# Attention over a key-value cache with a gated MLP: code order, head output and the place of one product

## The chip, the cores and the metric

The kernel runs on one core of a Trainium2 chip. The metric is the device time of one launch in microseconds (us), as the median of several runs. A profiled execution gives the trace that all views below come from.

## The reference

A decode step for two sequences (B = 2), one new token each, D = 512. Cut to what matters:

```python
xn = layernorm(x)
q  = (xn @ wq)                              # 32 query heads of 128
k, v = repeat(k_cache, 4), repeat(v_cache, 4)   # 8 kv heads, 32768 keys of 128
p  = softmax(q @ k.T * 128**-0.5)
s  = (p @ v) @ wo                           # [2, 1, 512]
h  = xn + shifted(gelu(layernorm(xn) @ w1)) @ w2
g  = silu(h + gelu(layernorm(h) @ w3) @ w4)
out = x + s * g
```

With one token per sequence the shifts fill everything with zeros, so the kernel needs neither w1 nor w2. All inputs are bf16. The caches are by far the largest: 8 MB of keys and 8 MB of values for each of the 16 pairs of a sequence and a kv head.

## The kernel before

The work goes in 16 groups, one for each pair (sequence, kv head). A group has four query heads. Its keys come in two halves (slots) of 128 partitions by 128 keys by 128 numbers; `kbuf` has three slots, `vbuf` two. SyncE issues all large transfers on one queue in a fixed order: the keys of the next group when the first half of this group's keys is used up (semaphore `s_half`), the values of the next group when this group's PV has ended (`s_pv`). After the last values come three parts of wo (`wo_parts`: heads 0-3, 4-6, 7), which land in `kbuf` beside the last keys.

The orders of the engines are written out by hand, and semaphores join them; `take` waits for a semaphore and counts it down. In a group:

- VectorE transposes the keys in 16 pieces into four buffers `T` (L481). A fifth transpose waits until TensorE has used the first buffer (`t_used`).
- TensorE multiplies each piece with the query in `z` (L550, 64 products into the banks `sc`).
- VectorE takes the peaks of the scores (`peak`, L464, L466), TensorE spreads them (L562), VectorE gives the negative shift (L493, L495), ScalarE the two exponentials with their sums `rs` (L411), VectorE transposes them into `pt` (L502) and puts the sums into `sm` (L499).
- TensorE adds the sums over the partitions (L566, a product with ones, `S`); then VectorE makes the denominators `den` and their reciprocals `rec` (L506, L510).
- TensorE multiplies the probabilities with the values (PV, L575, 64 products into `o`). Its result lies in four strips, with four blocks of columns in each.

The output of a head is made during the next group. `head_ob` on VectorE, after the fourth transpose, picks the right block of `o` with a mask `row_t` (L442) and adds the four blocks (L446) into `obm`; `head_oT` on TensorE (L526) turns it with one fp32 product; `head_on` on VectorE (L438) divides; `head_xp` on TensorE (L531) spreads it; `head_out` on VectorE (L451, L457, L458) makes a column of `oX`. The start of `head_ob` is released by SyncE (`t_o`), after it has issued the next values.

TensorE runs the 16 turns as a loop in its instruction stream with a counter `turn`. Its code consists of blocks, in memory in this order: `pe_turn` (a branch), `pe_groups` (a turn), `pe_prologue` (queries, MLP), `pe_next` (counts and branches back), `pe_output`. The output stage has the last head's `head_oT`, the 64 products of heads 0-3 with wo (L599), `head_xp`, and the 64 products of heads 4-7. Between the first 64 and `head_xp` it has a branch on `turn` whose target is named ahead by a prefetch hint at the stage's start (L586, L590). VectorE then multiplies with the gate and adds x (L517, L518), and SyncE and ScalarE store the result (L520). VectorE's 16 groups are a loop as well, two groups to a turn.

Of the kernel before, what the change touches and what calls it, by code (L numbers as in the profile page):

```python
# [7 lines left out]
F32 = mybir.dt.float32  # L8
# [86 lines left out]
def kernel(  # L95
# [43 lines left out]
    def sb(name, shape, dt):  # L139
        return pool.tile(shape, dt, name=name)  # L140
# [12 lines left out]
    den = sb("den", [128, rep], F32)  # L153
    obm = sb("obm", [128, Dh], F32)
    mx = sb("mx", [128, NPART], F32)
# [17 lines left out]
    sel_o = sb("sel_o", [128, VT, rep], F32)  # L173
    row_t = sb("row_t", [128, VT], F32)
    quad = sb("quad", [128, 4], BF16)
# [37 lines left out]
    def sem(name):  # L213
        return tc.alloc_semaphore(name)
# [14 lines left out]
    t_used, t_top, t_e, t_S, t_oT, t_xp = (sem(f"t_{n}") for n in ("used", "top", "e", "S", "oT", "xp"))  # L229
    t_d, t_o = sem("t_d"), sem("t_o")  # L230
    t_k = [sem(f"t_k{i}") for i in range(NPART)]
# [14 lines left out]
    with tc.tile_critical(no_gpsimd_drain=True):  # L246
# [15 lines left out]
        e_z0 = po.op(lambda e: e.memset(z[:, :, :, :], 0.0))  # L262
        e_g0 = po.op(lambda e: e.memset(g4[:, :], 0.0))
        for n in range(NQ):
            ac.op(lambda e, n=n: e.dma_start(out=x4_bf[32 * n:32 * n + B, :], in_=A_x[:, 0, n * QW:(n + 1) * QW]), e_x4z, inc=(d_x4, 16))


        ve.op(lambda e: e.memset(o[:, :], 0.0), inc=(t_o, 1))
        ve.op(lambda e: e.memset(pro[:, :], 0.0))
# [21 lines left out]
        for j in range(4):  # L291
# [5 lines left out]
            axis=AX.X, op=ALU.add))  # L297
        ve.op(lambda v: v.tensor_reduce(out=row_t[:, :], in_=sel_o[:, :, :], axis=AX.X, op=ALU.add), (ve.sem, ve.n))
        with nc.allow_low_precision(reason="one of the terms is one, the others are zero"):
# [88 lines left out]
        for m in range(1, NG):  # L388
            base = m % 2
            if m < NG - 1:  # L390
                sp.op(lambda e, m=m, base=base: e.dma_start(
                    out=kbuf[:, base * SLOT:(base + NPART) * SLOT], in_=row_view(A_k_cache, *groups[m])),
                    (s_half, m), e_q, inc=(t_k[0], 16))
                nc.sync.sem_inc(t_k[1], 16)
            else:
                for i, h in enumerate(order(m)):
                    sp.op(lambda e, m=m, h=h, base=base: e.dma_start(
                        out=kbuf[:, (base + h) * SLOT:(base + h + 1) * SLOT],
                        in_=row_view(A_k_cache, *groups[m])[:, h * SLOT:(h + 1) * SLOT]),
                        (s_half, m), inc=(t_k[i], 16))  # L400
            load_v(m, (s_pv, m))
            nc.sync.sem_inc(t_o, 1)
        for i, (a, c) in enumerate(wo_parts):
            sp.op(lambda e, a=a, c=c: e.dma_start(out=wo3[:, a:c, :], in_=wos[:, a:c, :]), (s_pv, NG - 1), inc=(d_wo[i], 16))
        sp.wait((s_pv, NG))
        nc.sync.sem_inc(t_o, 1)


        for m in range(NG):
            for i in range(NPART):  # L410
                ac.op(lambda v, i=i: v.activation(  # L411
                    out=ep[i][:, :], in_=sc[i][:, :], func=ACT.Exp, scale=inv_sqrt_dh, bias=shift[:, :], accum_out=rs[:, i:i + 1]),
                    (s_shift, m + 1), e_tf if m == 0 else None, inc=(t_e, 1))

        z_cols = z[:, :, :, (NR - 1) * rep:].rearrange("p n e c -> p (n e) c")
# [19 lines left out]

        def head_on():
            take(nc.vector, t_oT, 2)
            nc.vector.tensor_mul(out=on[:, :], in0=oT[:, :], in1=rec[:, :]).then_inc(t_on, 1)  # L438

        def head_ob():  # L440
            take(nc.vector, t_o)
            nc.vector.tensor_mul(  # L442
                out=ob[:, :].rearrange("p (t d) -> p t d", t=VT), in0=o[:, :].rearrange("p (t d) -> p t d", t=VT),
                in1=row_t[:, :].unsqueeze(2).broadcast_to([128, VT, Dh])).then_inc(t_d, 1)
            take(nc.vector, t_d)
            nc.vector.tensor_reduce(  # L446
                out=obm[:, :], in_=ob[:, :].rearrange("p (t d) -> p d t", t=VT), axis=AX.X, op=ALU.add).then_inc(t_ob, 1)

# [20 lines left out]

        ve.op(lambda v: v.memset(rec[:, :], 1.0), inc=(t_oT, 1))  # L470
        with nc.Fori(0, NG // 2, engines=[DVE], hint_back_edge=True):
            for par in range(2):
                for i, h in enumerate(order(par)):
# [3 lines left out]
                    for r in range(NR):  # L477
                        n = i * NR + r
                        if n >= T_BUFS:
# [3 lines left out]
                            in_=kt[:, r * W:(r + 1) * W].rearrange("p (t b k) -> p t b k", b=NB, t=RT)).then_inc(t_T, 1)  # L483
                        if i == 0 and r == 3:
                            head_ob()
                        if i == 1 and r == 3:
# [9 lines left out]
                for i, h in enumerate(order(par)):  # L496
                    take(nc.vector, t_e)
                    if i == NPART - 1:
# [5 lines left out]
                        in_=ep[i][:, :].rearrange("p (t r h) -> p t r h", r=NR, h=rep)).then_inc(t_pt, 1)  # L504
                take(nc.vector, t_S)
                nc.vector.tensor_reduce(  # L506
                    out=den[:, :], in_=S[:, 0:NPART * rep].rearrange("p (i h) -> p h i", h=rep),
                    axis=AX.X, op=ALU.add).then_inc(t_d, 1)
                take(nc.vector, t_d)
                nc.vector.reciprocal(out=rec[:, :], in_=den[:, :]).then_inc(t_oT, 1)  # L510
        head_ob()
        head_on()
# [11 lines left out]
        def head_oT():  # L524
            take(nc.tensor, t_ob)
            nc.tensor.matmul(oT[:, :], lhsT=obm[:, :], rhs=sel_h[:, :], start=True, stop=True).then_inc(t_oT, 1)  # L526

# [13 lines left out]
        with nc.body("pe_groups", valid_engines=[PE]):  # L541
            take(nc.tensor, t_z)
            for i in range(NPART):
# [21 lines left out]
            take(nc.tensor, t_pt, NPART)  # L565
            nc.tensor.matmul(  # L566
                S[:, 0:NPART * rep], lhsT=ones_f[:, :], rhs=sm[:, :, :].rearrange("p i h -> p (i h)"),
                start=True, stop=True).then_inc(t_S, 1)
            for h in range(NPART):
# [11 lines left out]
            ins.then_inc(s_pv, 1)  # L581
            nc.br("pe_next", engines=[PE])


        with nc.body("pe_output", valid_engines=[PE]):
            in_next_block = nc.tensor.mark_branch_hint_location()  # L586
            head_oT()
            for i, (a, c) in enumerate(wo_parts):
                if i == 1:
                    nc.tensor.br_ne(turn, 0, "pe_output_2", "pe_turn").branch_hint(in_next_block)  # L590
                    nc.switch_bb("pe_output_2")
                    head_xp()
# [13 lines left out]
        with nc.body("pe_prologue", valid_engines=[PE]):  # L606
            prologue.place()
            for s, v in prologue._new((e_s00, e_ones, e_const, e_hf, e_tf)):
                nc.tensor.wait_ge(s, v)
            nc.br("pe_next", engines=[PE])  # L610
        with nc.body("pe_next", valid_engines=[PE]):
            nc.regs_alu(turn, turn, 1, op=ALU.add)
            nc.br_lt(turn, NG + 1, on_true="pe_turn", on_false="pe_output", engines=[PE])
        nc.regs_mov(turn, 0)
# [32 lines left out]
```

## Time and profile before

| what | value |
|---|---|
| median of 3 runs | 661.88 us (661.82 to 662.24) |
| the profiled execution, its own time | 662.16 us |
| its span, first to last instruction | 660.0 us |
| mean granted TensorE clock | 0.828 |
| TensorE busy with products | 423.8 us (64%) |
| VectorE busy | 404.0 us (61%) |
| ScalarE busy | 29.6 us (4%) |
| moved by DMA | 280.57 MB, mean 425 GB/s |

The span is the time from the first to the last instruction that the profile shows; the profiled execution's own time is 2.16 us longer. Views give times in us from the start of the span. "Lnnn" is a line of the kernel before. An idle time stands with what ended it ("<-"); "issue" means that the engine waited for nothing that the profile shows. PEld is TensorE's weight load, and an engine's name with a q (SPq, DVEq) its sequencer.

### The profile page before, as it was taken

The numbers are of one execution on the slowest core, as the hardware profiler recorded it, in microseconds if no ns is written. First come the engines' busy times: TensorE is split into PE (matmuls) and PEld (weight loads), VectorE is DVE, ScalarE is ACT, GpSimd is POOL, SyncE is SP. The second block draws the span as 40 slices with busy tenths as digits, with TensorE's granted clock in tenths as the row PEclk, the third lists the DMA queues.
The fourth block names the chain that finished last, engine by engine and source line by source line (L and its number), as shares of the span: only waits on it lengthen the run. The fifth ranks groups of instructions, "written<-read, shape, count | busy, mean of one in ns | idle before, by whom it ended". The sixth has DMA issues, their size and how long they took to land. (4 is left out here: it accounts for less than half of the span.)

```text
span 660.0 us, 6591 instructions
## 1 busy us (share of the span) xinstructions
PE 423.8 (64%) x2412; PEld 151.6 (23%) x2412; DVE 404.0 (61%) x571; ACT 29.6 (4%) x72; POOL 9.7 (1%) x42
## 2 busy tenths in 40 slices
PE   1637396666739666684965668496566848656965
PEld 0112132222213222221321222132122213212323
DVE  5349293773929477392946739294673919468761
ACT  1100000000000000000000000000000000000000
POOL 1000000000000000000000000000000000000000
PEclk9859788796978879697877969677796977779897
DMA  8999999999999999999999999999999999999994
GB/s 361 442 438 441 445 437 421 417 445 441 445 433 417 425 445 441 441 429 422 429 445 441 441 421 429 429 445 441 437 425 429 429 445 441 433 425 419 435 414 167
DMA packets 6458, 280.57 MB, mean 425 GB/s; under 512 B 682, under 2 KB 692, under 8 KB 1716
## 3 DMA queue, kind: packets, MB, share of 16 engines
q1 hardware_dynamic: 6408, 280.50, 98.3%
q8 instruction: 2, 0.03, 0.0%
q14 instruction: 4, 0.03, 0.0%
q10 hardware_dynamic: 44, 0.01, 0.0%
HBM read 280.50 MB, written 0.00 MB: 425 GB/s over the span
## 5 line engine op out<-in xcount | busy, mean ns | idle before, releaser
L481 DVE STREAM_TRANSPOSE T<-kbuf 128x1024 int32<-128x1024 int32 x256 | 293.9, 1210 | 151.7 <-DVEq L461 151.7
L550 PE MATMUL sc<-T,z 128*128 128x512 bf16 x1024 | 295.8, 424 | 137.1 <-PEq L461 128.2
L550 PEld LDWEIGHTS sc<-T,z 128*128 128x128 bf16 x1024 | 92.6, 103 | 325.8 <-issue 268.0
L575 PE MATMUL o<-vbuf,pt 128*16 128x512 bf16 x1024 | 92.7, 542 | 0.0
L411 ACT ACTIVATE ep<-sc,shift 128x512 bf16<-128x512 f32 x32 | 21.7, 683 | 581.0 <-DVE shift L495 581.0
L575 PEld LDWEIGHTS o<-vbuf,pt 128*16 128x16 bf16 x1024 | 30.8, 119 | 54.2 <-issue 47.2
L566 PE MATMUL S<-sm,ones_f 128*128 128x8 f32 x32 | 9.0, 354 | 51.8 <-PEq L461 51.8
L502 DVE STREAM_TRANSPOSE pt<-ep 128x512 bf16<-128x512 bf16 x32 | 22.6, 708 | 15.3 <-DVEq L461 15.3
L464 DVE TENSOR_REDUCE mx<-sc 128x1 f32<-128x512 f32 x32 | 21.5, 672 | 15.7 <-DVEq L461 15.7
L562 PE MATMUL S<-mxr,same_h 128*128 128x64 f32 x32 | 6.5, 284 | 22.0 <-PEq L461 22.0
L566 PEld LDWEIGHTS S<-sm,ones_f 128*128 128x128 f32 x32 | 7.9, 307 | 53.5 <-issue 53.5
L446 DVE TENSOR_REDUCE obm<-ob 128x128 f32<-128x512 f32 x17 | 17.7, 1040 | 2.5
L442 DVE TENSOR_TENSOR ob<-o,row_t 128x512 f32<-128x512 f32 x17 | 11.2, 656 | 7.6 <-DVEq L461 7.6
L562 PEld LDWEIGHTS S<-mxr,same_h 128*128 128x128 f32 x32 | 4.8, 188 | 29.8 <-issue 29.8
L506 DVE TENSOR_REDUCE den<-S 128x4 f32<-128x8 f32 x16 | 2.7, 167 | 13.7 <-DVEq L461 13.7
L466 DVE TENSOR_SCALAR mxr<-row_of,mx 128x32 f32<-128x32 f32 x32 | 7.7, 241 | 4.8
L431 POOL COPY oX<-oXs 128x4 bf16<-128x4 bf16 x15 | 2.9, 191 | 517.6 <-DVE oXs L458 517.6
L493 DVE TENSOR_REDUCE top<-S 128x1 f32<-128x64 f32 x16 | 3.6, 224 | 11.2 <-DVEq L461 11.2
L526 PEld LDWEIGHTS oT<-sel_h,obm 128*128 128x128 f32 x34 | 6.3, 188 | 5.4 <-issue 2.7
L329 PE MATMUL sc<-kbuf,xT 128*2 128x512 bf16 x32 | 3.6, 627 | 5.5 <-DMA kbuf<-in_A_wq_dram 5.5
L366 PE MATMUL sc<-vbuf,h_bf 128*2 128x512 bf16 x14 | 4.9, 522 | 2.4 <-DVE h_bf L363 2.4
L420 POOL TENSOR_TENSOR z<-qr,quad 128x64 bf16<-128x64 bf16 x16 | 4.7, 294 | 107.6 <-DVE shift L495 90.4
(80 smaller groups left out, 73.8 us busy)
## 6 DMA issues: line engine op xcount, KB each, us to landing
kbuf<-in_A_k_cache_dram SPq DMA_DIRECT2D x2, 4096.0 KB, 22.0
vbuf<-in_A_v_cache_dram SPq DMA_DIRECT2D x2, 4096.0 KB, 18.6
kbuf<-in_A_wq_dram SPq DMA_DIRECT2D x1, 4096.0 KB, 13.5
vbuf<-in_B_w_dram SPq DMA_DIRECT2D x2, 1792.0 KB, 19.2
kbuf<-in_A_wo_dram SPq DMA_DIRECT2D x1, 2048.0 KB, 27.6
kbuf<-in_A_wo_dram SPq DMA_DIRECT2D x1, 1536.0 KB, 31.0
kbuf<-in_A_wo_dram SPq DMA_DIRECT2D x1, 512.0 KB, 31.7
kbuf<-in_A_k_cache_dram SPq DMA_DIRECT2D x15, 27.0
```

What stands on the lines that cost most here:

```text
L411: ac.op(lambda v, i=i: v.activation(out=ep[i][:, :], in_=sc[i][:, :], func=ACT.Exp, scale=inv_sqrt_dh, bias=shift[:, :], accum_out=rs[:, i ...
L442: nc.vector.tensor_mul(out=ob[:, :].rearrange("p (t d) -> p t d", t=VT), in0=o[:, :].rearrange("p (t d) -> p t d", t=VT), in1=row_t[:, :]. ...
L446: nc.vector.tensor_reduce(out=obm[:, :], in_=ob[:, :].rearrange("p (t d) -> p d t", t=VT), axis=AX.X, op=ALU.add).then_inc(t_ob, 1)
L464: nc.vector.tensor_reduce(out=mx[:, i:i + 1], in_=sc[i][:, :], axis=AX.X, op=ALU.max).then_inc(t_d, 1)
L466: ins = nc.vector.tensor_scalar_mul(out=mxr[:, i, :], in0=row_of[:, :], scalar1=mx[:, i:i + 1])
L481: nc.vector.transpose(out=Ts[n % T_BUFS][:, :].rearrange("p (b t k) -> p t b k", b=NB, t=RT), in_=kt[:, r * W:(r + 1) * W].rearrange("p (t ...
L502: nc.vector.transpose(out=pt[h][:, :, :].rearrange("p r (t h) -> p t r h", h=rep), in_=ep[i][:, :].rearrange("p (t r h) -> p t r h", r=NR, ...
L526: nc.tensor.matmul(oT[:, :], lhsT=obm[:, :], rhs=sel_h[:, :], start=True, stop=True).then_inc(t_oT, 1)
L550: ins = nc.tensor.matmul(sc[i][:, :], lhsT=z[:, nb, w, zc:zc + 128], rhs=Tb[:, nb, :, w], start=(r == 0 and nb == 0 and w == 0), stop=(r = ...
L562: nc.tensor.matmul(S[:, NPART * rep:], lhsT=same_h[:, :], rhs=mxr[:, :, :].rearrange("p i r -> p (i r)"), start=True, stop=True).then_inc( ...
L566: nc.tensor.matmul(S[:, 0:NPART * rep], lhsT=ones_f[:, :], rhs=sm[:, :, :].rearrange("p i h -> p (i h)"), start=True, stop=True).then_inc( ...
L575: ins = nc.tensor.matmul(o[32 * j:32 * j + VT * rep, :], lhsT=pt[h][:, r, a * VT * rep:(a + 1) * VT * rep], rhs=vt[:, u * VT:(u + 1) * VT, ...
```

## The change

TensorE's blocks are put in another order: the counting and the branch back stand at the end of `pe_groups`, `pe_output` follows, and the prologue comes last, ending with a count and a jump to `pe_turn`. The branch with its hint in the output stage is taken out.

The head's output goes another way: ScalarE copies all of `o` into `ob` as soon as PV has ended, and `head_oT` adds the four blocks with four fp32 products against the selection matrix `sel_o`. `head_ob`, `obm`, `row_t` and the semaphore `t_o` go, and SyncE's increments of it.

The sum of the exponentials (`S`) comes behind PV instead of ahead of it, and VectorE makes `den` and `rec` in `head_on`, in the next group, right before they are used. For the first group `S` and `ob` are filled by memsets.

```diff
+        po.op(lambda e: e.memset(ob[:, :], 0.0), inc=(t_ob, 1))
...
-        ve.op(lambda e: e.memset(o[:, :], 0.0), inc=(t_o, 1))
+        ve.op(lambda e: e.memset(o[:, :], 0.0))
+        ve.op(lambda e: e.memset(S[:, 0:NPART * rep], 1.0), inc=(t_S, 1))
...
-        ve.op(lambda v: v.tensor_reduce(out=row_t[:, :], in_=sel_o[:, :, :], axis=AX.X, op=ALU.add), (ve.sem, ve.n))
...
             load_v(m, (s_pv, m))
-            nc.sync.sem_inc(t_o, 1)
...
-        sp.wait((s_pv, NG))
-        nc.sync.sem_inc(t_o, 1)
...
+            ac.op(lambda v: v.copy(out=ob[:, :], in_=o[:, :]), (s_pv, m + 1), inc=(t_ob, 1))
...
         def head_on():
+            take(nc.vector, t_S)
+            nc.vector.tensor_reduce(
+                out=den[:, :], in_=S[:, 0:NPART * rep].rearrange("p (i h) -> p h i", h=rep),
+                axis=AX.X, op=ALU.add).then_inc(t_d, 1)
+            take(nc.vector, t_d)
+            nc.vector.reciprocal(out=rec[:, :], in_=den[:, :]).then_inc(t_oT, 1)
             take(nc.vector, t_oT, 2)
             nc.vector.tensor_mul(out=on[:, :], in0=oT[:, :], in1=rec[:, :]).then_inc(t_on, 1)
-
-        def head_ob():
...
-        ve.op(lambda v: v.memset(rec[:, :], 1.0), inc=(t_oT, 1))
...
-                        if i == 0 and r == 3:
-                            head_ob()
...
-                take(nc.vector, t_S)
-                nc.vector.tensor_reduce(
-                    out=den[:, :], in_=S[:, 0:NPART * rep].rearrange("p (i h) -> p h i", h=rep),
-                    axis=AX.X, op=ALU.add).then_inc(t_d, 1)
-                take(nc.vector, t_d)
-                nc.vector.reciprocal(out=rec[:, :], in_=den[:, :]).then_inc(t_oT, 1)
-        head_ob()
         head_on()
...
         def head_oT():
             take(nc.tensor, t_ob)
-            nc.tensor.matmul(oT[:, :], lhsT=obm[:, :], rhs=sel_h[:, :], start=True, stop=True).then_inc(t_oT, 1)
+            for t in range(VT):
+                ins = nc.tensor.matmul(
+                    oT[:, :], lhsT=ob[:, t * Dh:(t + 1) * Dh], rhs=sel_o[:, t, :],
+                    start=(t == 0), stop=(t == VT - 1))
+            ins.then_inc(t_oT, 1)
...
             take(nc.tensor, t_pt, NPART)
-            nc.tensor.matmul(
-                S[:, 0:NPART * rep], lhsT=ones_f[:, :], rhs=sm[:, :, :].rearrange("p i h -> p (i h)"),
-                start=True, stop=True).then_inc(t_S, 1)
...
             ins.then_inc(s_pv, 1)
-            nc.br("pe_next", engines=[PE])
+            nc.tensor.matmul(
+                S[:, 0:NPART * rep], lhsT=ones_f[:, :], rhs=sm[:, :, :].rearrange("p i h -> p (i h)"),
+                start=True, stop=True).then_inc(t_S, 1)
+            nc.regs_alu(turn, turn, 1, op=ALU.add)
+            nc.br_lt(turn, NG + 1, on_true="pe_turn", on_false="pe_output", engines=[PE])
...
         with nc.body("pe_output", valid_engines=[PE]):
-            in_next_block = nc.tensor.mark_branch_hint_location()
             head_oT()
             for i, (a, c) in enumerate(wo_parts):
                 if i == 1:
-                    nc.tensor.br_ne(turn, 0, "pe_output_2", "pe_turn").branch_hint(in_next_block)
-                    nc.switch_bb("pe_output_2")
                     head_xp()
...
-            nc.br("pe_next", engines=[PE])
-        with nc.body("pe_next", valid_engines=[PE]):
             nc.regs_alu(turn, turn, 1, op=ALU.add)
-            nc.br_lt(turn, NG + 1, on_true="pe_turn", on_false="pe_output", engines=[PE])
+            nc.br("pe_turn", engines=[PE])
```

More of the change, by code (lines that the diff above doesn't have):

```diff
@@ L153 @@
     den = sb("den", [128, rep], F32)
-    obm = sb("obm", [128, Dh], F32)
     mx = sb("mx", [128, NPART], F32)
@@ L173 @@
     sel_o = sb("sel_o", [128, VT, rep], F32)
-    row_t = sb("row_t", [128, VT], F32)
     quad = sb("quad", [128, 4], BF16)
@@ L229 @@
     t_used, t_top, t_e, t_S, t_oT, t_xp = (sem(f"t_{n}") for n in ("used", "top", "e", "S", "oT", "xp"))
-    t_d, t_o = sem("t_d"), sem("t_o")
+    t_d = sem("t_d")
     t_k = [sem(f"t_k{i}") for i in range(NPART)]
@@ L436, in head_on @@
         def head_on():
+            take(nc.vector, t_S)
[4 more added lines that the diff above has]
+            nc.vector.reciprocal(out=rec[:, :], in_=den[:, :]).then_inc(t_oT, 1)
             take(nc.vector, t_oT, 2)
             nc.vector.tensor_mul(out=on[:, :], in0=oT[:, :], in1=rec[:, :]).then_inc(t_on, 1)
-        def head_ob():
[L441 to L444, printed above, removed]
-            take(nc.vector, t_d)
-            nc.vector.tensor_reduce(
-                out=obm[:, :], in_=ob[:, :].rearrange("p (t d) -> p d t", t=VT), axis=AX.X, op=ALU.add).then_inc(t_ob, 1)
         def head_out(last=False):
@@ L504 @@
                         in_=ep[i][:, :].rearrange("p (t r h) -> p t r h", r=NR, h=rep)).then_inc(t_pt, 1)
-                take(nc.vector, t_S)
-                nc.vector.tensor_reduce(
-                    out=den[:, :], in_=S[:, 0:NPART * rep].rearrange("p (i h) -> p h i", h=rep),
-                    axis=AX.X, op=ALU.add).then_inc(t_d, 1)
-                take(nc.vector, t_d)
-                nc.vector.reciprocal(out=rec[:, :], in_=den[:, :]).then_inc(t_oT, 1)
-        head_ob()
         head_on()
```

## The prediction

> **What bounds the kernel now.** I read the page's DMA rows first, then SyncE's waits and the transfers by line, then the chain that ended last, then the time line of the last 50 us.
>
> ```profile
> DMA  8999999999999999999999999999999999999994
> GB/s 361 442 438 441 445 437 421 417 445 441 445 433 417 425 445 441 441 429 422 429 445 441 441 421 429 429 445 441 437 425 429 429 445 441 433 425 419 435 414 167
> q1 hardware_dynamic: 6408, 280.50, 98.3%
> q8 instruction: 2, 0.03, 0.0%
> ```
>
> The 16 DMA engines are busy in every slice but the last; 280.5 MB at some 430 GB/s are the time. Only what comes after the transfers, or what lets them pause, can move the end. (q8's two packets of 16 KB come back below.)
>
> ```profile
> SPq L380 <- PE o L575: 303.2, 14, 22.4
> SPq L391 <- PE sc L550: 209.1, 13, 16.8
> L380 SPq DMA_DIRECT2D vbuf<-in_A_v_cache_dram x15: 327/328/334, 30.2 to 577.8; - x15
> DMA to landing us min/median/max: 23.6/24.3/31.3
> L404 SPq DMA_DIRECT2D kbuf<-in_A_wo_dram x3: 388/507/4286, 618.5 to 619.5; - x3
> DMA to landing us min/median/max: 27.6/31.0/31.7
> ```
>
> A group's V is issued when the group before has ended its PV. Groups follow each other every 38.6 us, 19.3 us per 8 MB load, and the shortest issue-to-landing of V is 23.6 us: each V load stands at least 4.3 us in a queue that still has work (K: 26.9 - 19.3 = 7.6 us). So in steady state nothing that an engine does counts unless it delays a V issue by over 4.3 us. The three wo transfers land last: 618.53 + 27.6 = 646.1, 618.96 + 31.0 = 649.9, 619.51 + 31.7 = 651.2 us.
>
> ```profile
> 650.53 0.36 PE oT L526 x2
> 650.89 1.66 PE pro L599 x64
> 652.55 0.20 PE xp L531 x4
> 652.75 1.59 PE pro L599 x54
> 654.34 1.14 issue
> 655.47 0.35 PE pro L599 x10
> ```
>
> The end is TensorE's output stage: the last head's oT, 64 products, xp, 64 products, with a hole of 1.14 us six products into the last sixteen, which waits for no semaphore (the last wo part was there at 651.2, oX at 653.4). In the trace TensorE's second 16 KB instruction packet moves from 653.14 to 654.10: the hole is a code read.
>
> ```profile
> 612.26 4.62 DVE L481 STREAM_TRANSPOSE T<-kbuf 128x1024 int32<-128x1024 int32 x4 [0.46 <-DVEq L461]
> ...
> 617.49 3.79 PE L550 MATMUL sc<-T,z 128*128 128x512 bf16 x16
> ...
> 618.61 0.69 DVE L442 TENSOR_TENSOR ob<-o,row_t 128x512 f32<-128x512 f32 x1 [1.72 <-DVEq L461]
> 619.45 1.05 DVE L446 TENSOR_REDUCE obm<-ob 128x128 f32<-128x512 f32 x1
> 620.42 9.12 DVE L481 STREAM_TRANSPOSE T<-kbuf 128x1024 int32<-128x1024 int32 x8
> ...
> 641.90 6.42 PE L575 MATMUL o<-vbuf,pt 128*16 128x512 bf16 x64
> ```
>
> The last group begins at 612.26, right as its K lands; its PV waits for VectorE's chain, which stands still from 616.88 to 620.42 for head_ob. From 612 us on the compute chain, not the transfers, sets the end.
>
> **The change, part by part.** Steady state: each group loses head_ob on VectorE (587.85 to 589.60 in group 14: 1.75 us), gains den and rec inside head_on (0.17 + 0.18 us and two semaphore hops; from S's end at 641.97 to rec's end at 642.61: 0.64), and PV no longer waits for S (0.5 us, 641.41 to 641.90). V is issued some 1.6 us earlier; the cover is the full queue, so the gain there is nothing. Without it, each microsecond would count 15 times. ScalarE's copy waits for the PV and has the next exponentials queued behind it, 20 us later: nothing. The two semaphore increments leave SyncE's queue: nothing until the end. The new memsets: POOL's 128x512 before z, which is needed at 20.2 us; VectorE's S takes no more than row_t (0.17) gives back.
>
> The prologue moves to the end of TensorE's code. Its first product waits for xs_bf until 8.7 us. The jump to it now took place at 1.15 us and the first code packet was in at 5.15, so a read hides there. If not, V0's issue (30.23) moves, and K0 lands only at 42.3: some 12 us of cover. Nothing.
>
> Last groups: PV of group 14 comes 1.75 - 0.64 + 0.5 = 1.6 us earlier; S behind it holds TensorE 0.57 us, so group 15's scores start at 617.49 - 1.0 = 616.5. VectorE's fifth transpose then waits only for the first T buffer, four products of 0.24 us (3.79 / 16): 617.4. The ninth needs K's second half (595.16 + 26.7 = 621.9) and the four before it (617.4 + 4.6 = 622.0): 622.0 instead of 625.0. Then 5.56 us to the thirteenth (625.0 to 630.56) plus 0.64 for den and rec: 628.2 instead of 630.56, so 2.3 us earlier; I take 2.0, as scores at half clock (0.427 us each, 1.7 us a tile against VectorE's 1.14) would give some back. From there to PV is as before, less the 0.5 us of S: PV at 639.4, 6.42 us long, ends at 645.8. (Its second half needs V's at 617.98 + 23.2 = 641.2: there.)
>
> Head output: before, PV's end to oT's end is 648.32 to 650.89 = 2.57 us (semaphore through SyncE, 0.69 + 1.05 on VectorE, oT). After: no copy on ScalarE is in the trace; nearest is the exponential of the same 128x512 from PSUM, 0.683 us; below it VectorE's 0.65. I take 0.68. Four fp32 products are eight passes where two took 0.39 us, 0.11 apart: 0.39 + 6 x 0.11 = 1.05; at the most eight passes of S's half-clock load (0.29), unoverlapped, 2.3. I take 1.05, the same operation. With hops 0.15: oT ends at 645.8 + 0.68 + 1.05 + 0.15 = 647.7. S and den/rec (0.57 + 0.64) run beside copy and oT: nothing.
>
> Output stage: 64 products 1.66: 649.4; xp 0.2: 649.6; the next 48 wait for the second wo part, 649.93, and take 48 x 26.7 ns = 1.28: 651.25; the last 16 have their wo (651.16) and oX (649.6 + 0.85) and take 0.43: 651.7, against 655.83 now. So 4.1 us, and what is late next is the wo transfer itself, which this change doesn't touch. What follows the last product (655.83 to 660.0) stays.
>
> Sum: span 660.0 - 4.1 = 655.9; the profiled run took 662.16, 2.16 more than its span: 658.06. The median of the runs is 0.28 below that run: 657.8.
>
> These products run at a granted clock of 0.50 (651 to 654 us). [...]
>
> **Rivals.** *B, the code read stays, elsewhere.* Counting both programs, the output stage begins some 130 TensorE instructions earlier, since the prologue no longer lies before it. The code boundary of the hole then lies behind the stage, inside the prologue; the one before it may fall into the first 64 products. Its code shares a packet with the prologue's and is read at the start; it is missed only if it doesn't stay. Price: between the hole (1.14) and packet start to restart (655.47 - 653.14 = 2.33): 649.4 becomes 650.5 to 651.7, the end 652.4 to 653.6: 658.5 to 659.8. Against it: before, the loop, some 445 instructions from end to end, made 16 turns and no read appears between 4.14 and 653.14. [...]
>
> *C, the last PV doesn't move* (scores at half clock hold VectorE up). Then 648.3 + 1.9 = 650.2; 1.66 + 0.2 + 1.28 + 0.43 on it: 653.8, a gain of 2.05: 659.8. Against it: the clock was 1.0 from 616.9 to 640.8.
>
> *D, slower: the far jumps throw the loop's code out, and each back edge reads it again.* Price of a read, jump to arrival, from the start: 1.15 to 5.15, 4.0 us; two reads 8.0; TensorE's sequencer reaches the back edge 2.45 us before PV ends (614.92, 617.37), so 5.5 us per turn. The queue's 4.3 and the 1.6 gained hide it in steady state; in the last turn it lies on the path whole, with B's hole: 657.8 + 5.5 + 1.2 = 664.5. It decides from a stall of 4.1 us a turn. For it: the jump to the prologue now passes loop and output. Against it: the loop itself shrinks from about 445 instructions to 313, and showed no read.
> [...]
>
> *E, no gain:* a wait that I overlooked holds the output until some 655 us: 661.9.
>
> **How the numbers follow.** Forecast 0.60, B 0.17, C 0.10, D 0.08, E 0.05. A measurement of this kernel tells about 0.2%, 1.3 us. Forecast, B and C are all faster by more: 0.86; within it 0.06; slower 0.08. Low end: 657.8 less 0.2 (full clock) and 0.4 (the spread of the runs): 657.2. High end: C with the same spread, 660.2. D and E stay out.
>
> **What would show it.** Right: last transfers landing near 651.2 as before; PV's last end near 645.8; ScalarE's copy near 0.68; oT's eight passes near 1.05 us; products of pro waiting for DMA at 650 to 651; no hole; last product near 651.7; 4.2 us behind it. Wrong: an "issue" hole in the output (B), PV's last end still at 648 (C), more q8 packets and gaps at back edges (D), or a transfer that ends later than 651.2, which would move everything.

## The result and the profile after

| | before | after |
|---|---|---|
| median, run side by side | 661.85 us (661.33 to 662.24) | 659.07 us (657.85 to 659.97, 6 runs) |
| profiled execution, its own time | 662.16 us | 659.43 us |
| its span | 660.0 us | 657.6 us |

The ratio is 0.9958, 95% interval 0.9945 to 0.997: 2.8 us faster. Sign and range were right; the forecast gain was 4.1 us. The profiled execution ended 1.37 us later than its forecast of 658.06.

The page of the kernel after, the rows of the DMA engines and of the two queues (packets, MB, share of 16 engines):

```profile
DMA  8999999999999999999999999999999999999995
q1 hardware_dynamic: 6408, 280.50, 98.8%
q8 instruction: 7, 0.11, 0.1%
```

The DMA engines are as busy as before, and the loads are the same 280.50 MB. But q8, which brings code, carried seven packets of 16 KB instead of two. The trace has them at 2.07, 8.99, 30.68, 30.81, 74.37, 653.12 and 657.36 us; before, at 4.14 and 653.14.

The chain that ended last in the kernel after (start, duration, what):

```profile
618.78 33.92 DMA kbuf<-in_A_wo_dram
652.71 0.14 issue
652.84 0.42 PE pro L585 x16
```

Before, this chain was TensorE's output stage with a hole of 1.14 us in it. Now it is the last wo transfer with sixteen products behind it: 0.14 + 0.42 us. The transfer, which was expected at 651.2 as before, landed at 652.7.

The time line of the kernel after, in its last group (start, duration, engine, line, work; in brackets the idle time before it and what ended it):

```profile
623.66 4.62 DVE L474 STREAM_TRANSPOSE T<-kbuf 128x1024 int32<-128x1024 int32 x4 [0.71 <-DVEq L455]
...
631.33 5.56 PE L538 MATMUL sc<-T,z 128*128 128x512 bf16 x16 [0.99 <-PEq L455]
...
642.06 5.58 PE L560 MATMUL o<-vbuf,pt 128*16 128x512 bf16 x64 [3.39 <-PEq L455]
...
647.69 0.59 ACT L410 COPY ob<-o 128x512 f32<-128x512 f32 x1 [6.86 <-PE o L560]
648.42 1.03 PE L511 MATMUL oT<-sel_o,ob 128*128 128x4 f32 x8 [0.46 <-PEq L455]
649.38 1.06 PE L585 MATMUL pro<-kbuf,oX 128*2 128x128 bf16 x64
651.62 0.84 PE L585 MATMUL pro<-kbuf,oX 128*2 128x128 bf16 x48 [0.99 <-DMA kbuf<-in_A_wo_dram]
652.84 0.39 PE L585 MATMUL pro<-kbuf,oX 128*2 128x128 bf16 x16 [0.38 <-DMA kbuf<-in_A_wo_dram]
```

The head's new way is seen from 647.69 on: a copy of 0.59 us on ScalarE, eight passes of 1.03 us, then products that twice wait for wo. No hole remains. The last PV begins at 642.06, as before (641.90) and not at the forecast 639.4. VectorE's ninth transpose started at 623.66, since K's second half landed at 623.4 instead of 621.9. Four tiles later the scores ran in part at half clock (granted 0.50 from 632.4 to 635.8; 5.56 us where 4.44 was usual).

Where does the lateness begin? In the traces a load lands in 16 shares (one for each of the 16 DMA engines, as the author reads it), and what waits for it starts behind the last: VectorE's first transpose at 44.02 after a last share at 43.9, before at 42.41 after 42.3. Shares of the first K (group 0), in us:

| kernel | first share | 13th | 14th | 15th | last |
|---|---|---|---|---|---|
| before | 40.5 | 41.2 | 41.3 | 41.7 | 42.3 |
| after | 40.5 | 41.7 | 42.3 | 43.6 | 43.9 |

Two shares stand out, right after two code packets that came at once, at 30.68 and 30.81 us, and took 1.61 and 2.04 us (the one at 74.37 took 0.92). From there every landing stays late: the three wo parts ended at 647.7, 651.5 and 652.7, before at 646.1, 649.9 and 651.2. The DMA row shows no pause between its first and its last slice (90% or more in each), and nothing gave the lateness back. Of the 1.55 us at the end, 1.28 are this spread of the shares; the first share of the last wo part came only 0.27 us later than before (650.04 and 649.77).

### The profile page after: what moved, and what is told of

Its sections match the earlier page's. It is cut to its first block, busy times and chain, and to the rows that moved or that the text cites. A ratio compares the mean times of both kernels' runs of the same rounds, so it can differ in the third digit from the quotient of the medians.

```text
span 657.6 us, 6698 instructions
## 1 busy us (share of the span) xinstructions
PE 411.0 (62%) x2498; PEld 165.8 (25%) x2514; DVE 376.7 (57%) x538; ACT 38.9 (6%) x88; POOL 10.2 (2%) x43
## 3 DMA queue, kind: packets, MB, share of 16 engines
q1 hardware_dynamic: 6408, 280.50, 98.8%
HBM read 280.50 MB, written 0.00 MB: 427 GB/s over the span
## 5 line engine op out<-in xcount | busy, mean ns | idle before, releaser
L538 PE MATMUL sc<-T,z 128*128 128x512 bf16 x1008 | 280.1, 427 | 141.2 <-PEq L455 137.1
L538 PEld LDWEIGHTS sc<-T,z 128*128 128x128 bf16 x1024 | 100.8, 105 | 300.8 <-issue 220.0
L560 PE MATMUL o<-vbuf,pt 128*16 128x512 bf16 x1024 | 90.3, 530 | 54.2 <-PEq L455 54.2
L560 PEld LDWEIGHTS o<-vbuf,pt 128*16 128x16 bf16 x1024 | 32.5, 116 | 106.2 <-issue 98.6
L511 PEld LDWEIGHTS oT<-sel_o,ob 128*128 128x128 f32 x136 | 17.7, 191 | 3.2 <-issue 0.5
L511 PE MATMUL oT<-sel_o,ob 128*128 128x4 f32 x136 | 16.2, 242 | 0.5 <-PEq L455 0.5
L410 ACT COPY ob<-o 128x512 f32<-128x512 f32 x16 | 9.4, 586 | 110.8 <-PE o L560 110.8
L519 PE MATMUL xp<-on,sel_r 128*128 128x4 bf16 x68 | 4.1, 164 | 5.2 <-PEq L455 5.0
L567 PEld LDWEIGHTS S<-sm,ones_f 128*128 128x128 f32 x32 | 4.8, 188 | 6.9 <-issue 6.9
L407 ACT ACTIVATION_READ_ACCUMULATOR ep<-sc,shift 128x1 f32 x32 | 6.3, 196 | 0.0
## 6 DMA issues: line engine op xcount, KB each, us to landing
kbuf<-in_A_k_cache_dram SPq DMA_DIRECT2D x15, 28.6
```

The source lines that it names most:

```text
L407: ac.op(lambda v, i=i: v.activation(out=ep[i][:, :], in_=sc[i][:, :], func=ACT.Exp, scale=inv_sqrt_dh, bias=shift[:, :], accum_out=rs[:, i ...
L410: ac.op(lambda v: v.copy(out=ob[:, :], in_=o[:, :]), (s_pv, m + 1), inc=(t_ob, 1))
L511: ins = nc.tensor.matmul(oT[:, :], lhsT=ob[:, t * Dh:(t + 1) * Dh], rhs=sel_o[:, t, :], start=(t == 0), stop=(t == VT - 1))
L538: ins = nc.tensor.matmul(sc[i][:, :], lhsT=z[:, nb, w, zc:zc + 128], rhs=Tb[:, nb, :, w], start=(r == 0 and nb == 0 and w == 0), stop=(r = ...
L560: ins = nc.tensor.matmul(o[32 * j:32 * j + VT * rep, :], lhsT=pt[h][:, r, a * VT * rep:(a + 1) * VT * rep], rhs=vt[:, u * VT:(u + 1) * VT, ...
L567: nc.tensor.matmul(S[:, 0:NPART * rep], lhsT=ones_f[:, :], rhs=sm[:, :, :].rearrange("p i h -> p (i h)"), start=True, stop=True).then_inc( ...
```

## The experiments

Three questions: does the missing 1.3 us come from the code reads (theory R: they travel on the engines that carry the loads, and an engine set behind sets every landing) or from the head's new way (H)? Which part of the change carries the gain? And is the wo transfer the floor of what is left, and the early V issue of value (theory Q)? Ratios are to the kernel before, run on the same chip; "kernel 3" is the kernel of experiment 3.

**1. The change with the code order and the hint of before.**

```diff
-            nc.regs_alu(turn, turn, 1, op=ALU.add)
-            nc.br_lt(turn, NG + 1, on_true="pe_turn", on_false="pe_output", engines=[PE])
+            nc.br("pe_next", engines=[PE])
...
+            in_next_block = nc.tensor.mark_branch_hint_location()
...
+                    nc.tensor.br_ne(turn, 0, "pe_output_2", "pe_turn").branch_hint(in_next_block)
...
+            nc.br("pe_next", engines=[PE])
+        with nc.body("pe_next", valid_engines=[PE]):
```

> The changed kernel with TensorE's code in the order of before (prologue between loop and output, hint in the output stage). Theory R (code reads share DMA engines with the loads; each 16 KB read makes an engine late, and the latest engine sets every landing): one code packet before 640 us as before, K of group 0 fully landed at 42.3 us (43.9 in the changed kernel), last wo at 651.2 (652.7); the hole of 1.1 us in the output is back. Last product 652.0 to 653.0, run 658.2 to 659.2. Rival H (the transfers are late by 1.5 us from the head's new way: the memsets, ScalarE's copy): K of group 0 at 43.9 and wo at 652.7 as in the changed kernel, and with the hole on top a run of 660 us or more.

Measured: 658.10 us (657.71 to 658.56), before 661.59; ratio 0.9947 (0.9933 to 0.996). Time line and chain of this kernel:

```profile
639.52 5.95 PE L560 MATMUL o<-vbuf,pt 128*16 128x512 bf16 x64 [3.39 <-PEq L455]
646.25 1.03 PE L511 MATMUL oT<-sel_o,ob 128*128 128x4 f32 x8 [0.46 <-PEq L455]
650.20 0.84 PE L587 MATMUL pro<-kbuf,oX 128*2 128x128 bf16 x48 [1.75 <-DMA kbuf<-in_A_wo_dram]
```

```profile
617.15 34.15 DMA kbuf<-in_A_wo_dram
...
651.43 0.62 PE pro L587 x15
```

Only two code packets before 640 us (4.2, 31.0), and wo is there at 651.3. All of the forecast's chain is found here: PV at 639.52 (639.4 forecast), oT's end 647.28 (647.7), the last product 652.03 (651.7). H falls: the new head is in this kernel whole. A hole that the old order might have brought back did not come.

**2. The new code order alone, in the kernel before** (the same lines turned round).

> The kernel before with only the new order of TensorE's code and no hint. Theory R: six code packets before 640 us or so, K of group 0 landed at 43.9, wo at 652.7; the last group's chain starts 1.5 us later, the hole of 1.14 is gone: the sum is about nothing, 661.5 to 662.5. Rival H: K of group 0 at 42.3, wo at 651.2, and only the hole is gone: 660.6.

Measured: 661.48 us (659.37 to 663.15, 12 runs); ratio 1.0 (0.9985 to 1.0014). By itself the order is worth nothing. A half miss: the hole was gone (in the chain the second 64 products, one of them missing in the trace, have no break), but the stream was not late: the first K's last share came at 42.3, wo at 651.4, as before. The code packets were at 2.1, 8.7, 30.8 and 74.4, each by itself. So it isn't their number; what the change has beyond these is the second packet at 30.8.

```profile
652.95 1.81 PE pro L597 x63
```

The last product was 1.1 us earlier than before, the span 0.9 us shorter (659.1); the runs scatter over 3.8 us, more than that.

**3. The change with the prologue ahead of the loop**, so that no far jump is left.

```diff
-        with nc.body("pe_turn", valid_engines=[PE]):
-            nc.br_ne(turn, 0, on_true="pe_groups", on_false="pe_prologue", engines=[PE])
...
-            nc.br_lt(turn, NG + 1, on_true="pe_turn", on_false="pe_output", engines=[PE])
+            nc.br_lt(turn, NG, on_true="pe_groups", on_false="pe_output", engines=[PE])
...
-        with nc.body("pe_prologue", valid_engines=[PE]):
-            prologue.place()
...
+        prologue.place()
...
+        nc.br("pe_groups", engines=[PE])
```

> The changed kernel with the prologue at the start of TensorE's code, straight before the loop, so that nothing jumps but the loop's back edge. Theory R: at most two code packets before 640 us, K of group 0 at 42.3, last wo at 651.2 to 651.8. The output's end lies in a code block of its own, read late: a hole of up to 1 us some 45 products into the second 64. Run 657.7 to 659. If the back edge now crosses too many blocks: reads in every turn, and a run above 662. Rival H: K of group 0 at 43.9, run 659 or more.

Measured: 657.74 us (657.63 to 658.36); ratio 0.9942 (0.9928 to 0.9955), faster than the kernel before. Against the change's 0.9958 (0.9945 to 0.997) the two intervals just overlap; experiments 4 and 8 come out at the same time as this one. Page and chain:

```profile
q8 instruction: 3, 0.05, 0.0%
```

```profile
617.22 34.05 DMA kbuf<-in_A_wo_dram
```

The first K ended at 41.7, wo at 651.3, 1.4 us earlier than in the change, and the last product at 651.99.

**4. The same with padding.** The 120 register moves that were to be the padding became one instruction (the trace has a single one, as in 3), so this is a repeat of 3.

> [...] Theory R: two or three code packets before 640 us, K of group 0 at 42.3 to 42.9, no hole, last product at 651.7 to 652.3, run 657.5 to 658.3. Rival: where code lies doesn't matter for the reads and the run is as that of the unpadded one within 0.3 us.

Measured: 657.77 us (657.45 to 657.97). Nothing on padding follows; it shows how well such a time repeats.

**5. The change again**, unaltered.

> The changed kernel once more, unaltered, beside its variants on one chip. Theory R: again five code packets or so before 640 us, last wo later than the 651.3 us of the kernels with the prologue first or in its old place (652 to 653), and runs that scatter by 2 us with a median of 658.7 to 659.3, about 1.3 us above those. Rival: the first measurement was an accident of its chip, and the change with its own code order measures 657.8 as they do.

Measured: 658.12 us (657.83 to 659.9), ratio 0.9945 (0.9926 to 0.9963), below the expected 658.7 to 659.3. Its profiled execution took 659.9 us, again with a pair of code packets at 30.8 (1.80 and 1.92 us long), the first K at 44.1 and wo at 653.1. The twelve runs of the change fall into two groups: seven of 657.83 to 658.7, and five of 659.43 to 659.97. Both profiled ones are of the later group and have the pair. So the late stream is not in every run. That the earlier runs are those where the reads miss the loads is argued, not shown: none of them has a trace.

**6. Far jumps at the end of turns 1 to 13** (prologue ahead of the loop, and a jump over 1200 instructions and back).

```diff
+            nc.br_eq(turn, NG, on_true="pe_output", on_false="pe_mid", engines=[PE])
...
+        with nc.body("pe_mid", valid_engines=[PE]):
+            nc.br_lt(turn, 14, on_true="pe_far1", on_false="pe_groups", engines=[PE])
...
+        with nc.body("pe_far2", valid_engines=[PE]):
+            nc.regs_mov(scr, 0)
+            nc.br("pe_groups", engines=[PE])
```

> The kernel with the prologue first, where TensorE, at the end of each of the turns 1 to 13, jumps through a block behind the output and one more than 600 instructions further, and back. PV of the next group has some 6 us of idle time ahead of it there. Theory R: two or more code packets per turn, 26 or more in all; 16 KB cost an engine about 0.6 us of its share (64 KB take 2.42 us): if they fall on the same one or two engines, the last wo lands 8 to 16 us late, and the run is 666 to 674; if they are spread over all engines, 1 us late, 659. Rival H (code reads cost the loads nothing): last wo at 651.3, run 657.8.

Measured: 660.17 us (659.38 to 661.4, 10 runs); ratio 0.9975 (0.9961 to 0.9989). A miss as a test: instead of 26 reads there were five packets before the end (64.8, 76.6, 83.7, 83.9, 93.6). In the first turn the two far jumps stopped TensorE's sequencer for 6.95 and 8.49 us; in the twelve turns behind it no branch took over 0.23 us. So a block once read stayed, for 13 turns of far jumps. The V that landed next, at 99 us, had its first share where kernel 3 had it and its last 1.5 us later. But the stops also put off the issue of the V behind it, by 5.0 us against kernel 3, so in the final time two causes are mixed. Two of the five packets came at once here too (1.45 and 2.03 us long). Experiment 11 repeats this with the V in the queue long before.

**7. The head's output as before, S behind PV** (prologue ahead of the loop; the lines are against kernel 3).

```diff
-            ac.op(lambda v: v.copy(out=ob[:, :], in_=o[:, :]), (s_pv, m + 1), inc=(t_ob, 1))
...
+        def head_ob():
...
+                        if i == 0 and r == 3:
+                            head_ob()
...
-            for t in range(VT):
-                ins = nc.tensor.matmul(
...
+            nc.tensor.matmul(oT[:, :], lhsT=obm[:, :], rhs=sel_h[:, :], start=True, stop=True).then_inc(t_oT, 1)
```

> The kernel with the prologue first, with the head's output as before (mask and sum on VectorE, one fp32 product, SyncE's increments) and the exponentials' sum still behind PV. The head's new way was worth 1.75 us on VectorE in the last group and 0.75 us behind PV, of which the wait for wo swallows 1.8: PV at 641.3, first 64 products end at 650.9 or so, last product 652.9, run 658.4 to 659.2. Rival (the gain is all from the head's output): 660 or more.

Measured: 662.61 us (660.45 to 666.53, 12 runs), ratio 1.0028 (1.0007 to 1.0049): slower than before, where 658.4 to 659.2 was expected. The chain:

```profile
654.48 1.28 issue
655.76 0.31 PE pro L595 x8
```

And from its time line in the last group:

```profile
620.10 0.69 DVE L449 TENSOR_TENSOR ob<-o,row_t 128x512 f32<-128x512 f32 x1 [1.56 <-DVEq L468]
620.94 1.05 DVE L453 TENSOR_REDUCE obm<-ob 128x128 f32<-128x512 f32 x1
...
631.90 0.16 DVE L439 TENSOR_REDUCE den<-S 128x4 f32<-128x8 f32 x1
632.21 0.18 DVE L443 RECIPROCAL rec<-den 128x4 f32<-128x4 f32 x1
...
644.64 5.12 PE L570 MATMUL o<-vbuf,pt 128*16 128x512 bf16 x64 [3.44 <-PEq L468]
```

PV began at 644.64, three microseconds behind the expected 641.3: VectorE's chain now carries head_ob, den and rec together. The stream was 1.5 to 2 us late as well, and the hole of the kernel before came back, 1.28 us after 56 products. With the old head, then, nothing of the gain is left; experiment 8 leaves out the other part.

**8. The head's output as in the change, S, den and rec as before** (prologue ahead of the loop).

```diff
+            nc.tensor.matmul(
+                S[:, 0:NPART * rep], lhsT=ones_f[:, :], rhs=sm[:, :, :].rearrange("p i h -> p (i h)"),
+                start=True, stop=True).then_inc(t_S, 1)
...
-            nc.tensor.matmul(
-                S[:, 0:NPART * rep], lhsT=ones_f[:, :], rhs=sm[:, :, :].rearrange("p i h -> p (i h)"),
-                start=True, stop=True).then_inc(t_S, 1)
```

> The kernel with the prologue first, with the exponentials' sum ahead of PV and den and rec at the turn's end, as before. PV starts 0.5 us later against the peak, but den and rec no longer stand in VectorE's chain (0.64): PV at 639.4, as now. The chain has 1.8 us to spare before the second wo part. Run 657.6 to 657.9, no difference. Rival: the sum on PV's path counts, 658.3 or more.

Measured: 657.94 us (657.75 to 658.11); ratio 0.9939 (0.9921 to 0.9957). The chain:

```profile
617.08 34.23 DMA kbuf<-in_A_wo_dram
...
651.44 0.62 PE pro L583 x12
```

Moving S is worth nothing: PV at 639.24, wo at 651.3, as in 3. Together with experiment 7: the gain is the head's output.

**9. No wait for the later wo parts** (prologue ahead of the loop; heads 4 to 7 are multiplied with the first part of wo instead of theirs; the transfers are still made).

```diff
-                    pe.wait(e_s0, e_oX[(B - 1) * Hkv + k], (d_wo[i], 16))
+                    pe.wait(e_s0, e_oX[(B - 1) * Hkv + k], (d_wo[0], 16))
...
-                                pro[32 * n:32 * n + B, 0:QW], lhsT=oX[:, k, r, :], rhs=wo3[:, k, col:col + QW],
+                                pro[32 * n:32 * n + B, 0:QW], lhsT=oX[:, k, r, :], rhs=wo3[:, k % 4, col:col + QW],
```

> The kernel with the prologue first; the products of heads 4 to 7 take the first wo part instead of their own (wrong numbers), so that they wait for no later part; all parts are still loaded, and SyncE waits for them at the very end. Theory: the last wo part's landing (651.3) is what ends last after the change, so without it the chain of engines sets the end: first 64 products end at 648.3, xp, oX and the last products some 1.7 us later, last product 649.8 to 650.3, 2 us earlier; span 654.0 to 654.4, run 655.6 to 656.1. Rival: the chain itself is as late as the transfers, and the run stays within 0.5 us of 657.8.

Measured: 656.15 us (655.5 to 656.55), before 661.35; ratio 0.9912 (0.9888 to 0.9936). The chain has no DMA any more:

```profile
647.04 1.03 PE oT L511 x8
648.07 0.99 PE pro L583 x64
...
649.25 1.12 PE pro L583 x64
```

The wait for wo costs kernel 3 657.74 - 656.15 = 1.6 us, and in the traces the last product comes at 650.34 instead of 651.99: the transfer is the floor of kernel 3, and the chain of engines is 1.6 us ahead of it.

**10. V issued later** (prologue ahead of the loop; SyncE issues the next V only behind the head's copy and three more on ScalarE; in the trace that is 2.4 us behind PV's end, where it was 0.05).

```diff
-            load_v(m, (s_pv, m))
+            load_v(m, (s_late, m))
...
+            if m < NG - 1:
+                for _ in range(3):
+                    e_late = ac.op(lambda v: v.copy(out=spare[:, :], in_=o[:, :]), e_late)
+                nc.scalar.wait_ge(*e_late).then_inc(s_late, 1)
```

> The kernel with the prologue first, where SyncE issues V only after ScalarE has made three more copies of the same 128x512 behind the head's (some 2.1 us), and nothing else waits for them. The V issue then comes 1.4 to 2 us before the first of the 16 shares of K lands, instead of 3.7. Theory Q (the cover of the V issue was nearly used up before, and runs of kernels with under 3 us of it scatter and are late): the wo lands 1 to 4 us later than 651.3, the median is 659 to 662 and the runs scatter by over 1.5 us. Rival: any cover above zero is enough, the run is 657.8 with a scatter below 1 us.

Measured: 663.96 us (662.07 to 665.62), ratio 1.0038 (1.0017 to 1.006): 6.2 us slower than 3, more than expected. The V transfers of this kernel, and below them those of kernel 3:

```profile
L381 SPq DMA_DIRECT2D vbuf<-in_A_v_cache_dram x15: 327/328/328, 27.4 to 582.6; - x15
DMA to landing us min/median/max: 21.9/23.7/33.8
```

```profile
L379 SPq DMA_DIRECT2D vbuf<-in_A_v_cache_dram x15: 327/328/328, 28.4 to 577.8; - x15
DMA to landing us min/median/max: 24.8/25.8/32.6
```

Issue to landing is 2.1 us shorter at the median, so V stood that much less in the queue, and the last V was issued 4.8 us later. What counts, as the author reads it, is the time from V's issue to the first share of the K ahead of it, when one of the engines has nothing else left: median 4.6 us in kernel 3 (at least 3.7), 2.5 here (at least -0.5). Where it was below zero, the next V's first share came 2.3 us later than the usual 19.3 us behind that K; the nine other times under 3 us cost 0 to 0.5 us each. wo landed at 655.2, 4.0 us later than in kernel 3. Theory Q holds.

**11. Code reads before the loop** (prologue ahead of the loop, then three jumps over 800 waits each, where the expectation speaks of 400 instructions; the head and the loop are those of kernel 3).

```diff
+        for f in range(3):
+            with nc.body(f"pe_far{f}", valid_engines=[PE]):
+                nc.regs_mov(scr, 0)
+                nc.br_ne(scr, 0, on_true=f"pe_pad{f}", on_false=f"pe_far{f + 1}" if f < 2 else "pe_groups", engines=[PE])
+            with nc.body(f"pe_pad{f}", valid_engines=[PE]):
+                for _ in range(800):
+                    nc.tensor.wait_ge(s_pv, 1)
+                nc.br(f"pe_far{f + 1}" if f < 2 else "pe_groups", engines=[PE])
```

> The kernel with the prologue first, where TensorE, between prologue and loop, jumps through three blocks that lie 400 instructions apart each, in the idle time before the first K lands; the loop and the output lie behind them. Theory R: three or more additional code packets between 25 and 42 us; the first share of group 0's K still lands at 40.5, the last at 43 to 45 instead of 41.7, and stays late to the end: last wo 652.5 to 654, run 659 to 661. Rival H: K's last share at 41.7 to 42, wo at 651.3, run 657.8.

Measured: 659.54 us (659.37 to 660.06, 9 runs), ratio 0.9969 (0.9956 to 0.9982), against 657.74 of kernel 3. Its page's code row, and from its chain the transfer and the products behind it:

```profile
q8 instruction: 7, 0.11, 0.1%
```

```profile
618.01 33.75 DMA kbuf<-in_A_wo_dram
...
651.89 1.19 PE pro L583 x48
653.13 0.62 PE pro L583 x16
```

The second part of wo, which this chain ends in, landed at 651.76 (650.0 in kernel 3). Seven code packets, where kernel 3 has three: packets at 28.6, 35.7, 42.8, 43.0, 52.4 and 76.5, against 71.9 and 115.5 in kernel 3; those at 42.8 and 43.0 took 1.63 and 2.09 us. Each of the three jumps stopped TensorE's sequencer, for 6.48, 7.17 and 8.45 us. The shares of the first V tell what the packets did: the first at 59.7 (59.8 in kernel 3), the last at 63.3 (61.0). This V was issued at 28.9, before the first K had landed, so the queue had work throughout, and its last share still came 2.3 us late. At the end wo's last part landed at 653.0, 1.7 us later than in kernel 3, and the time is 1.8 us longer.

Head and loop are the same, so theory R is borne out at this V: code reads alone put single shares back by as much as the change lost (the last by 2.3 us, the first not at all; the change's last wo share by 1.55). The engine behind each share is the author's reading. One thing came along: the jumps also put off the issues of the next K (by 4.15 us) and the next V (2.7). They stand behind this V in the queue, so its 2.3 us aren't theirs. In the 1.7 us at the end they probably have a part: there the first share of wo's last part is 0.84 us late too (650.34 instead of 649.50), so only the other half is single late shares. The first share of that next V, issued 2.1 us ahead of the first share of its K instead of 4.7, was the first to be late, by 0.5 us.

The traces sharpen R, if the last share of a load is set against its first. In all four with two code packets at once (the change twice, 6, 11) it came 3.3 to 3.6 us behind the first in the load that they met. Single packets put the last share back too, but less: in kernels 3, 4 and 7 to 10, where the first K's last share was 1.1 to 1.5 us behind, it was 1.8 to 2.0 us behind after the single packets between 55 and 77 us, hardly more than the 1.7 to 1.9 us with which the kernel before and kernels 1 and 2 begin. In experiment 11 the first K, which met two single packets, ended at 42.58 instead of kernel 3's 41.68 (43 to 45 had been expected), so 0.9 of V's 2.3 us was there before the two at once. Why two at once cost so much more than one after the other stays open.

## Why the prediction was right or wrong

**The bound and the place of the gain: right.** The stream sets the time, and what was won was won in the last group. Steady state gave nothing.

**The cover of a V issue, 4.3 us: mis-sized.** The working takes it from the last share, as the shortest way from issue to landing less one load; by that, kernel 3 has 24.8 - 19.3 = 5.5 us, and the 2.4 us of experiment 10 should have cost nothing. They cost 6.2 us. Counted to the first share of the K ahead, as in experiment 10, V was issued 2.8 to 4.1 us ahead in the kernel before. In the change it was 2.3 to 4.6, and only the shortest of these put the next V back by more than 0.2 us (by 0.4).

**The head's output: right, and the sizes too.** Copy 0.586 us (0.68 taken), eight passes 1.03 (1.05), last PV to oT's end 647.64 to 649.45 = 1.8 (2.57 before, 1.9 forecast). With kernel 1 the moved PV and the chain behind it are right to 0.5 us. Experiments 7 and 8 show that this part carries the gain.

**What is late next: right.** The forecast named the wo transfer, and the chain ends in it; experiment 9 prices that wait, in kernel 3, at 1.6 us.

**"The prologue moves ... Nothing": the step that failed**, and with it "the last transfers near 651.2 as before". The working asked only whether TensorE waits for its code. It did, for 3.6 us (the first branch, 1.14 to 4.74), and that was hidden, as forecast. Left out was that code reads put shares of the loads back: five packets before the output stage where there was one, two of them at once. The last wo share, 652.71 instead of 651.16, is 1.55 us; the last product, 653.26 instead of 651.7, the same 1.56. The rest of the sum (what follows the last product 4.34 instead of 4.17, what lies outside the span 1.83 instead of 2.16) gives back 0.2: together the 1.37 us by which the profiled execution missed. The text had this case only in its last half sentence, without a price or a chance.

**S behind PV: right.** The working gives PV 0.5 us for it and takes 0.64 for den and rec on VectorE: 0.14 us lost. Experiment 8 has it at 0.3: kernel 3 has PV at 639.54 with the move, kernel 8 at 639.24 without. Neither shows in the time.

**The half-clock scores: allowed for, but with too little.** 2.0 instead of 2.3 us was taken for them. In the change one tile group took 5.56 instead of 4.44 us (the granted clock was 0.5 from 632.4 to 635.8), and VectorE then waited 2.10 us; with K's 1.5 us this puts PV at 642.06. It cost nothing of its own, since wo came later still.

**The products' clock: full, as the low end had it; why is not shown.** The first 64 took 1.06 us in the kernel after, 1.74 in the same view before; the granted clock was 1.0 from 646.05 to 656.29 us, and before it was 0.5 from 651.01 to 654.43. In the change it rose 4.0 us after PV's start. TensorE's pause behind PV was short there (0.46 us ahead of oT, 2.2 before), but in experiment 7 it was 1.9 us, nearly as long as before, and the 64 products took 1.06 us too. As the first 64 are followed by the wait for wo, they brought no time. The last sixteen took 0.39 us in the change, and 0.59 and 0.60 in kernels 1 and 3, whose pages have a granted clock of 0.7 in the last slice where the change has 0.8. No run shows the 0.2 us that the low end takes off for a full clock: against the forecast's 0.43 the last sixteen won 0.04.

**The rivals.** B (the read in the output stage): not seen, no hole in the change nor in kernels 1, 2 and 3, and no run shows that a code boundary lies in the first 64 products; experiment 7, with the old head, has a hole behind 56 products of the second 64. C (PV stays at 648): PV's end was 647.64, so its step came true, but only 1.1 us of the 2.7 by its own cause, the half-clock scores, and 1.5 by the late K; its end at 659.8 is near the measured one by chance, since kernels 1 and 3 have PV early and the change's last product waited for wo. D: its premise is half there, more reads, but none at the back edges: no packet from 74.37 to 653.12. Its price of a read, 4.0 us, was low: the far jumps of experiments 6 and 11 stopped TensorE's sequencer for 6.5 to 8.5 us each. Experiment 6 speaks against D too: 13 turns of far jumps, five packets in all, and no branch over 0.23 us behind the first turn. E: not seen.

## What to carry to other kernels

In this kernel, whose DMA engines are 90% busy or more in all slices but the first and the last, code placement is part of the DMA budget: with the prologue ahead of the loop there were three code packets instead of seven, and wo was there at 651.3 instead of 652.7. So put what is executed once in a straight line ahead of the loop, and compare the packets of the instruction queue in both traces before calling a jump free. Of a load that lands in 16 shares, read the first and the last; here a late last share (43.9 instead of 42.3) with an unmoved first one (40.5) pointed to the code packets. When a compute tail is shortened, look at the transfer behind it as the next floor; the versions with the prologue ahead of the loop (657.74 and 657.94 us) stand on it, and in the first of them the wait for it costs 1.6 us.

## What the runs showed of the hardware

- Some 64 KB of code more, two packets of it at once, moved the last landing of 280 MB by 1.7 us (experiment 11 against 3), about half of it as single late shares. A packet of 16 KB by itself mostly took about 0.95 us (0.88 to 1.01 in five of the seven single ones of the kernels before and after), and one or two such moved the last share by 0.5 to 0.9 us where it wasn't late yet; two at once took 1.4 to 2.1 us each, and the last share was then 3.3 to 3.6 us behind the first. A data packet of 64 KB took 2.42 (the median of 3840 in the kernel before).
- Code that had been read stayed: in none of the thirteen traces is there a code packet between 115.5 us and the output stage, though TensorE's loop makes 16 turns of some 310 to 445 instructions, and in experiment 6 thirteen of them had far jumps. The first passage of such a jump stopped TensorE's sequencer for 6.5 to 8.5 us (experiments 6 and 11), a later one for 0.2.
- The time by which V's issue is ahead of the first share of K goes with the scatter of the runs: kernels with a median of 4.5 us or more (1, 3, 4, 8, 9) lie within 1.1 us, those with 2.5 to 3.4 (before, 2, 7, 10) spread over 3.6 to 6.1 us; the change, with 3.7 and 3.2 in its two traces, over 2.1. Experiments 6 (4.7, but once 0.5) and 11 (3.7) spread over 2.0 and 0.7. The steady kernels have 4 to 6 runs each, kernels 2 and 7 twelve and the kernel before sixty, of which the first six lie within 0.9; so part of the difference may be the number of runs. Experiment 10 shows that a late issue costs time; that it makes the scatter is argued.
